# Two attention chunks ahead of the first weights, a planner that knows a shared port, and two small experts that end in one scatter

## The chip, the cores and the metric

The kernel runs on one core of a Trainium2 chip. Its engines are TensorE (PE; its weight loads are listed as PEld), VectorE (DVE), ScalarE (ACT), GpSimd (POOL) and SyncE (SP), which issues most transfers. Times are device microseconds of one execution; lower is better.

## The reference

Three stages run one after the other over 2304 rows of 512 numbers.

```python
# 1: attention with keys and values pooled by 8 (4 batches, 8 heads, 576 rows, 64 wide)
k_p = k.reshape(B, H, Sp, 8, D).mean(axis=3); v_p = v.reshape(B, H, Sp, 8, D).mean(axis=3)
attn = softmax(q @ k_p.T / 8); x = attn @ v_p           # as (2304, 512)
# 2: dense feed-forward, 512 -> 2048 -> 512
h = x @ w_in; r = np.maximum(h, 0.0); x = (r * r) @ w_out
# 3: eight experts, 512 -> 1024 -> 512; a row goes to the one with the largest logit
logits = x @ w_gate; e = argmax(logits); gate = softmax(logits)[e]
out[i] = gate[i] * (np.maximum(x[i] @ w1[e], 0.0) @ w2[e])   # first `capacity` rows of an expert; 0 for others
```

## The kernel before

**Precision.** Every large product is made from two parts of an operand, a high part rounded to the matrix format and the low rest: high by high, high by low, low by high. So each weight tile of stage 2 (32 tiles, 0 to 15 of `w_in`, 16 to 31 of `w_out`) has to be converted once, in `conv`: three steps on ACT (L265, L271, L287), three on DVE (L274 sign, L281 merge, L290 low). DVE's L290 is the last step; after it the tile can be used.

**Stages 1 and 2** work in nine chunks of 256 rows. In a chunk, attention makes scores (L412), a softmax, transposes (L499, L504) and the product with the values (L535, called av below). Stage 2 then has 16 pairs: a first-layer product `h` (L607, twelve matmuls with four `w_in` tiles), a square split into high and low (the low part on POOL, L627), and a second-layer product `y` (L640, twelve matmuls with one `w_out` tile). Chunks 0 and 1 go through stage 2 side by side, since the weights are being converted meanwhile; from chunk 2 on all weights are there.

**What sets the order.** The steps of stages 1 and 2 are not written in order. `add` records each with a priority, an engine, a cost in ns, what it reads and writes, and the buffers it takes. `Steps.run` then plays the engines through with these costs: each time it takes the step that can start earliest, the one of lowest priority number among equals, out of the first 80 of an engine's list. The order in which it took them is the order of the instructions on each engine, and each engine keeps it. A cost only decides the order; it is not a time on the chip.

**Pools at the start.** Keys are pooled on DVE (L320), laid out by ACT into `kT` (`k_place`, L363), values are pooled on DVE (L342) or, if named in `FOLD`, on POOL by three adds (L347, L348).

**The end.** After the large experts come two experts with at most 32 rows each, handled together in `twins`: `ga` makes the first layer (32 matmuls in four groups, L1446), `h_sum` turns half of it round by matmuls and relu (L1460, L1462, L1463), `gc` makes the second layer (32 matmuls, L1470), `end` scales by the gate (ACT L1481, DVE L1482) and writes the rows to their places by an indirect transfer of GpSimd, a scatter (L1485), one for each expert.

Of the kernel before, what the change touches and what calls it, by code (L numbers as in the profile page):

```python
# [58 lines left out]
COLD = 20000  # L59
FIRST = 2 * 2 * NF  # L60
PLAN_AT, W_AT, LOG7_AT = 0, 1, 6
BACK = ((3, 12, 1), (5, 12, 1))
CST2 = (6, 20)
V0_LOAD = -70
CONV_LOAD = (-30, -30, -30, -30)
# [40 lines left out]
class Step:  # L106
    def __init__(self, prio, eng, cost, fn, lat):
        self.prio, self.eng, self.cost, self.fn, self.lat = prio, eng, cost, fn, lat
        self.deps, self.bufs, self.end, self.free = set(), [], None, None


class Steps:
# [9 lines left out]
    WINDOW = 80  # L122

    def __init__(self, room, slow):
        self.room, self.slow = room, slow
        self.taken = {p: [] for p in room}
        self.steps, self.writer, self.readers = [], {}, {}

    def add(self, prio, eng, cost, fn, r=(), w=(), u=(), lat=0):
        s = Step(prio, eng, cost, fn, lat)  # L130
        for x in (*r, *w):
            if x in self.writer:
                s.deps.add(self.writer[x])
# [32 lines left out]
    def run(self):  # L166
# [6 lines left out]
        while any(todo.values()):  # L173
# [21 lines left out]
            now[e] = s.free = t + s.cost * (2 if e == "PE" and t < self.slow else 1)  # L195
# [5 lines left out]
def tile_kernel(ctx: ExitStack, tc: tile.TileContext, q, k, v, w_in, w_out, w_gate, w1, w2, cap, gate_rows, consts, out):  # L201
# [38 lines left out]
    S_ = Steps(pools, COLD)  # L240
# [8 lines left out]
    def conv(i, prio, load_prio):  # L249
# [43 lines left out]
        add(load_prio, "SP", 1320, load, w=(raw,), lat=2300)  # L293
# [5 lines left out]
        add(prio, "DVE", 605, low, r=(cv, ("W", i, 0)), w=(("W", i, 1),))  # L299
# [11 lines left out]
    def k_pool(b, x, prio, load_prio, tag=None):  # L311
# [12 lines left out]
        add(load_prio, "SP", 740, load, w=(buf,), lat=2300)  # L324
# [5 lines left out]
    def v_pool(b, i, prio, load_prio, tag=None):  # L330
# [19 lines left out]
        add(load_prio, "SP", 660 * n // P, load, w=(buf,), lat=2300)  # L350
        if ("v", b, i) in FOLD:
            add(prio, "POOL", 1600, fold, r=("ap",), w=(buf, ("v", i)))
        else:
            add(prio, "DVE", 603, pool, r=(buf, "ap"), w=(("v", i),))

    def k_place(b, prio):

        pairs = kT.rearrange("p (x a s) -> p x a s", a=2, s=SP)
        r = tuple(("kd", x) for x in range(NPAIR))

        def place(a):
            h = slice(64 * a, 64 * a + 64)
            nc.scalar.activation(out=pairs[h, :, a], in_=kd[h], func=AF.Copy, scale=1.0 / 64.0)  # L363
# [34 lines left out]
    def a_scores(c, j, prio, qprio):  # L398
# [55 lines left out]
        add(qprio, "SP", 660 * n // P, load, w=(qT,), lat=2300)  # L454
# [30 lines left out]
        if (c, j) in NORM_DVE:  # L485
            add(prio(4), "DVE", 663, lambda: norm(nc.vector), r=((mxb, 2),), w=((ex, 0), (ex, 1)), u=(mxb, ex))
        else:
            add(prio(4), "POOL", 1450 if c < 3 else 1200, lambda: norm(nc.gpsimd), r=((mxb, 2),), w=((ex, 0), (ex, 1)), u=(mxb, ex))
# [105 lines left out]
    def g1(c, ff, prio):  # L594
# [57 lines left out]
        add(prio + 1, "POOL", 1000 if c < 2 else 720, low, r=(rb, ghb), w=(glb,))  # L652
# [254 lines left out]
    def rows_of_two(cols):  # L907
# [3 lines left out]
        for e, col in enumerate(cols):  # L911
            src = idxt[0:QP, bass.ds(col, 1)]
            nc.vector.tensor_scalar_add(out=cur[0:QP, e:e + 1], in0=src, scalar1=-1.0)
            for a in range(2):
                o = slice((2 * e + a) * QP, (2 * e + a + 1) * QP)
                nc.vector.tensor_scalar(out=gix[o, 0:1], in0=src, scalar1=-1.0, scalar2=0.0, op0=ALU.add, op1=ALU.max)

# [200 lines left out]
    add(-100, "DVE", 600, start_up, w=(("kT", 0), ("kT", 1)))  # L1118
# [7 lines left out]
    for i in range(5):  # L1126
        v_pool(0, i, V0_AT, V0_LOAD, f"W{22 + i}")
# [30 lines left out]
    for c in range(NCH):  # L1158
# [34 lines left out]
        if c == NCH - 2:  # L1193
# [21 lines left out]
            add(at, "PE", 500, lambda c=c: logit_mm(c), r=(("yts", 0), ("yts", 1), "wg4"), w=(g7,), u=(yt, lgb[c]))  # L1215
# [212 lines left out]
    def twins(hooks):  # L1428
# [8 lines left out]
        sidx, gate = begin(2)  # L1437
# [3 lines left out]
        def ga(half):  # L1441
            for e in range(2):
                ps = pp.tile([P, 512], F32, tag="h", name=f"ha{half}{e}", bufs=2)
                for kk in range(KD):
                    for x in range(2):
                        nc.tensor.matmul(  # L1446
                            ps, yc[kk // 2][:, kk % 2], ws[e][2 * kk + half][:, x],
                            start=(kk == 0 and x == 0), stop=(kk == KD - 1 and x == 1),
                        )
                o = slice(HP * e, HP * e + HP)  # L1450
                if e == 0:
                    nc.scalar.copy(out=hs[half][o], in_=ps[o])
                else:
                    nc.vector.tensor_copy(out=hs[half][o], in_=ps[o])
                hook(2 * half + e)
# [11 lines left out]
        def gc(e, half):  # L1467
            for fi in range(4 * half, 4 * half + 4):
                for x in range(2):
                    nc.tensor.matmul(  # L1470
                        py[e], hx[:, fi].rearrange("p e a t -> p (e a t)"), ws[e][8 + fi][:, x],
# [3 lines left out]
        def end(e, parts):  # L1475
            hi, lo = slice(HP * e, HP * e + QP), slice(HP * e + QP, HP * e + HP)
            ot, tt = hs
            n = DM // parts
            for i in range(parts):
                c = slice(i * n, i * n + n)  # L1480
                nc.scalar.activation(out=tt[hi, c], in_=py[e][lo, c], func=AF.Copy, scale=gate[lo, 0:1])  # L1481
                nc.vector.scalar_tensor_tensor(  # L1482
                    out=ot[hi, c], in0=py[e][hi, c], scalar=gate[hi, 0:1], in1=tt[hi, c], op0=ALU.mult, op1=ALU.add
                )
            nc.gpsimd.indirect_dma_start(  # L1485
                out=out, out_offset=bass.IndirectOffsetOnAxis(ap=sidx[0:QP, e:e + 1], axis=0), in_=ot[hi], in_offset=None,
                bounds_check=NTOK - 1, oob_is_err=False,
            )
# [274 lines left out]
```

## Time and profile before

| what | us |
|---|---|
| median of 3 runs | 693.34 (692.79 to 693.70) |
| the profiled execution | 694.46 |
| its span, first to last instruction | 692.70 |
| PE busy in the span | 662.9 (96%) |
| DVE, ACT, POOL busy | 422.0, 324.9, 190.6 |

The profiled execution is 1.76 us longer than its span. PE is the engine to watch: what it does not spend on matmuls, about 30 us, lies mostly at the start and at the end. The mean shares of the others say little here, since DVE is full in one stage and half idle in the rest.

### The profile page before, as it was taken

The numbers are of one execution on the slowest core, as the hardware profiler recorded it, in microseconds if no ns is written. First come the engines' busy times: TensorE is split into PE (matmuls) and PEld (weight loads), VectorE is DVE, ScalarE is ACT, GpSimd is POOL, SyncE is SP. The second block draws the span as 40 slices with busy tenths as digits, with TensorE's granted clock in tenths as the row PEclk, the third lists the DMA queues.
The fourth block names the chain that finished last, engine by engine and source line by source line (L and its number), as shares of the span: only waits on it lengthen the run. The fifth ranks groups of instructions, "written<-read, shape, count | busy, mean of one in ns | idle before, by whom it ended". The sixth has DMA issues, their size and how long they took to land. (4 is left out here: it accounts for less than half of the span.)

```text
span 692.7 us, 11860 instructions
## 1 busy us (share of the span) xinstructions
PE 662.9 (96%) x4195; PEld 593.3 (86%) x4196; DVE 422.0 (61%) x1119; ACT 324.9 (47%) x903; POOL 190.6 (28%) x231
## 2 busy tenths in 40 slices
PE   3799999999999999999999999999999999999995
PEld 3678889999898889898898999998997979989983
DVE  5899998322279899375289647445363646464451
ACT  3897785344254243345344344243432546454351
POOL 3244433232233233234233132242202111302111
PEclk9899999999999999999999999999999999999999
DMA  9997902310122320010010000062005664553110
GB/s 311 398 400 242 312 17 68 99 63 16 61 108 64 87 77 9 1 38 19 13 48 17 2 31 1 2 226 80 1 32 185 219 222 155 190 190 130 49 58 3
DMA packets 40970, 73.46 MB, mean 106 GB/s; under 512 B 8449, under 2 KB 17921, under 8 KB 40768
## 3 DMA queue, kind: packets, MB, share of 16 engines
q1 hardware_dynamic: 38496, 64.89, 27.6%
q0 software_dynamic: 2400, 7.66, 3.4%
q8 instruction: 37, 0.61, 0.4%
q14 instruction: 37, 0.30, 0.1%
HBM read 59.63 MB, written 13.05 MB: 105 GB/s over the span
## 5 line engine op out<-in xcount | busy, mean ns | idle before, releaser
L607 PE MATMUL h<-xh,W 128*128 128x256 f32 x1152 | 213.8, 284 | 1.4 <-DVE W L290 0.8
L627 POOL TENSOR_TENSOR gl<-r,gh 128x256 fp32r<-128x256 f32 x144 | 117.2, 814 | 289.5 <-ACT gh L623 194.0
L607 PEld LDWEIGHTS h<-xh,W 128*128 128x128 f32 x1152 | 184.4, 189 | 11.7 <-DVE W L290 1.0
L640 PE MATMUL y<-W,gh 128*128 128x512 f32 x576 | 185.3, 402 | 1.3 <-DVE W L290 1.3
L607 PE MATMUL h<-xl,W 128*128 128x256 f32 x576 | 161.6, 281 | 0.2 <-DVE xl L545 0.2
L619 DVE SCALAR_TENSOR_TENSOR r<-h,r 128x256 f32<-128x256 f32 x141 | 59.1, 419 | 101.8 <-ACT r L612 101.4
L640 PE MATMUL y<-W,gl 128*128 128x512 f32 x288 | 113.8, 395 | 0.8 <-POOL gl L627 0.7
L640 PEld LDWEIGHTS y<-W,gh 128*128 128x128 f32 x576 | 99.2, 189 | 17.0 <-DVE W L290 1.9
L607 PEld LDWEIGHTS h<-xl,W 128*128 128x128 f32 x576 | 108.9, 189 | 0.4 <-DVE xl L545 0.4
L623 ACT CAST gh<-r 128x256 fp32r<-128x256 f32 x144 | 58.6, 407 | 100.1 <-DVE r L619 96.8
L612 ACT ACTIVATE r<-h 128x256 f32<-128x256 f32 x144 | 55.1, 382 | 101.2 <-PE h L607 90.0
L1334 PE MATMUL hp<-yh,W 128*128 128x256 f32 (+1 forms) x384 | 74.5, 291 | 1.1 <-issue 1.1
L697 DVE SCALAR_TENSOR_TENSOR junk<-ysb,wgb 128x512 bf16<-128x512 f32 x80 | 66.3, 829 | 1.4
L640 PEld LDWEIGHTS y<-W,gl 128*128 128x128 f32 x288 | 54.2, 188 | 14.6 <-POOL gl L627 2.0
L1334 PEld LDWEIGHTS hp<-yh,W 128*128 128x128 f32 x384 | 61.1, 188 | 1.8 <-issue 1.3
L1303 PE MATMUL po<-W,xh_e 128*128 128x512 f32 x192 | 61.4, 401 | 0.0
L1334 PE MATMUL hp<-yl,W 128*128 128x256 f32 (+1 forms) x192 | 55.7, 290 | 0.0
L233 DVE TENSOR_TENSOR W<-stg,W 128x512 fp32r<-128x512 f32 x64 | 42.3, 689 | 12.2 <-ACT W L232 11.2
L1303 PEld LDWEIGHTS po<-W,xh_e 128*128 128x128 f32 x192 | 34.7, 188 | 6.8
L1340 DVE SCALAR_TENSOR_TENSOR xl_e<-hp,xh_e 128x256 fp32r<-128x256 f32 x48 | 20.2, 422 | 31.8 <-ACT xh_e L1339 31.6
L535 PE MATMUL av<-aT,vz 128*128 128x256 f32 (+3 forms) x192 | 38.5, 352 | 0.9 <-ACT aT L509 0.9
L1292 POOL DMA_INDIRECT out_dram<-ysb,sidx x12 | 11.9, 994 | 97.5 <-ACT ysb L1281 83.1
(204 smaller groups left out, 901.4 us busy)
## 6 DMA issues: line engine op xcount, KB each, us to landing
stg<-in_moe_w_dram SPq DMA_DIRECT2D x40, 512.0 KB, 4.7
raw<-in_moe_w_in_dram SPq DMA_DIRECT2D x16, 512.0 KB, 8.3
raw<-in_moe_w_out_dram SPq DMA_DIRECT2D x16, 512.0 KB, 8.6
kraw<-in_k_dram SPq DMA_DIRECT2D x16, 288.0 KB, 3.0
out_dram<-zt SPq DMA_DIRECT2D x18, 256.0 KB, 4.6
y_dram<-ysb SPq DMA_DIRECT2D x18, 256.0 KB, 2.1
qT<-in_q_dram SPq DMA_DIRECT2D x16, 256.0 KB, 2.7
vraw<-in_v_dram SPq DMA_DIRECT2D x16, 256.0 KB, 3.9
```

The lines of the kernel that those rows point to most:

```text
L233: eng.tensor_tensor(out=lo, in0=src, in1=f(hi), op=ALU.subtract)
L535: nc.tensor.matmul(ps[:, g], vz[:, cm].rearrange("p r d -> p (r d)"), abox["aT"][:, blk, :n], start=(x == 0), stop=(x == 1),)
L607: nc.tensor.matmul(ps, wt[kk][:, l, o:o + P], r[:, kk, :], start=(n == 0), stop=(n == 3 * KD - 1))
L612: nc.scalar.activation(out=box["r"], in_=box["ps"], func=AF.Relu)
L619: nc.vector.scalar_tensor_tensor(out=r, in0=box["ps"], scalar=0.0, in1=r, op0=ALU.max, op1=ALU.mult)
L623: nc.scalar.copy(out=box["gh"], in_=box["r"])
L627: nc.gpsimd.tensor_tensor(out=box["gl"], in0=box["r"], in1=f(box["gh"]), op=ALU.subtract)
L640: nc.tensor.matmul(st["y", c][t], l[:, ts], r, start=(ff == 0 and n == 0), stop=(ff == NF - 1 and n == 2))
L697: nc.vector.scalar_tensor_tensor(out=junk, in0=st["yb", c, t] if c < 2 else st["ysb", c][t], scalar=1.0, in1=st["wgb"][:, e], op0=ALU.mult ...
L1303: nc.tensor.matmul(ps, l, r, start=(fi == 0 and x == 0), stop=(fi == 7 and x == 2))
L1334: nc.tensor.matmul(ps, ww[:, l, o], r[:, kk, 0:n2], start=(kk == 0 and x == 0), stop=(kk == KD - 1 and x == 2))
L1340: nc.vector.scalar_tensor_tensor(out=lo, in0=p_, scalar=0.0, in1=f(h), op0=ALU.max, op1=ALU.subtract)
```

## The change

The planner gets a clock for PE that falls after a pause and comes back after steady work, and lengthens a step of DVE or POOL that runs beside one of the other (for the DVE steps marked `port`). Costs are changed to suit. The attention of chunk 1 gets priorities ahead of all weights, the score products wait for their half of `kT` only, and no values are folded on POOL. `twins` puts one group of the first layer behind `h_sum(0)`, makes the second expert's result in two column halves in separate PSUM tiles, and writes both experts with one scatter over 96 partitions, of which 32 hold an index of -1 and write nothing.

```diff
-V0_LOAD = -70
-CONV_LOAD = (-30, -30, -30, -30)
+V0_LOAD = (-96,) * 5
+CONV_LOAD = (-50,) * 4
-CH1 = (0, 2, 0.5)
+CH1 = (-30, 6, 0.5)
-Q0 = {(0, 0): -98.5, (0, 1): -97, (1, 0): -50, (1, 1): -50}
-FOLD = [('v', 0, 2), ('v', 0, 3), ('v', 0, 4)]
+Q0 = {(0, 0): -98.5, (0, 1): -97, (1, 0): -95, (1, 1): -94}
+FOLD = []
...
-            now[e] = s.free = t + s.cost * (2 if e == "PE" and t < self.slow else 1)
+            cost = s.cost
+            if e == "PE":
+                if t > now[e] + self.COOL:
+                    self.warm = False
+                if t > now[e] + self.GAP:
+                    self.since = t
+                if t > self.since + self.WARM_UP:
+                    self.warm = True
+                cost *= 1 if self.warm else 2
+            if s.port:
+                o = {"DVE": "POOL", "POOL": "DVE"}[e]
+                if self.port[o] > t:
+                    cost += min(cost, self.port[o] - t) * self.SHARE[e]
+                self.port[e] = t + cost
...
-        add(prio, "DVE", 600, sign, r=(raw,), w=(cv,))
-        add(prio, "DVE", 700, merge, r=(raw,), w=(cv,))
+        add(prio, "DVE", 340, sign, r=(raw,), w=(cv,), port=True)
+        add(prio, "DVE", 605, merge, r=(raw,), w=(cv,), port=True)
...
+        parts = [slice(0, 2), slice(2, NPAIR)] if b == 0 else [slice(0, NPAIR)]
-        for a in range(2):
-            add(prio, "ACT", 450, lambda a=a: place(a), r=(*r, "ap"), w=(("kT", a), "kT in"))
+        for xs in parts:
+            cells = [g for g in range(2) if xs.start <= 2 * g < xs.stop]
+            for a in range(2):
+                w = [x for g in cells for x in (("kT", a, g), ("kT in", g))]
+                add(prio, "ACT", 450 // len(parts), lambda a=a, xs=xs: place(a, xs), r=(...), w=w)
...
-        def end(e, parts):
+        left, right = slice(0, DM // 2), slice(DM // 2, DM)
+        right_of_b = pp.tile([P, DM // 2], F32, tag="sc", name="pb", bufs=2)
+        sums = [(0, slice(0, DM), py[0]), (1, left, py[1][:, left]), (1, right, right_of_b)]
+        def end(i, tt):
...
-        ga(0)
-        ga(1)
+        ga(0, 0)
+        ga(0, 1)
+        ga(1, 0)
         h_sum(0)
+        ga(1, 1)
         gc(0, 0)
         h_sum(1)
         gc(1, 0)
+        gc(2, 0)
         gc(0, 1)
-        end(0, 1)
+        end(0, hs[1])
         gc(1, 1)
-        end(1, 2)
+        end(1, hs[1])
+        gc(2, 1)
+        end(2, yg[:, 0])
+        n = HP + QP
+        nc.gpsimd.indirect_dma_start(
+            out=out, out_offset=bass.IndirectOffsetOnAxis(ap=sidx[0:n, 0:1], axis=0), in_=hs[0][0:n], in_offset=None,
+            bounds_check=NTOK - 1, oob_is_err=False,
+        )
```

How the order of the instructions moves, at three places. On PE, from the end of chunk 1's scores to the first stage-2 product (in `ata_1_0` the first number is the chunk, the second the row tile; `h_0_0` is chunk 0, pair 0; the last number is a buffer), before:

```order
L412 MATMUL sc_1_1_0_189<-kT_86,qT_1_1_131 128x144 x2
L412 MATMUL sc_1_1_1_196<-kT_86,qT_1_1_131 128x144 x2
L499 MATMUL ata_0_0_211<-cst_60,ex_0_0_140 128x128 x4
L504 MATMUL atb_0_0_222<-cst_60,ex_0_0_140 128x128
L499 MATMUL ata_0_1_239<-cst_60,ex_0_1_161 128x128 x4
L504 MATMUL atb_0_1_249<-cst_60,ex_0_1_161 128x128
L535 MATMUL av_0_0_0_262<-aT_0_0_229,vz_89 128x256 x4
L535 MATMUL av_0_0_2_279<-aT_0_0_229,vz_89 128x256 x4
L607 MATMUL h_0_0_310<-xh_0_260,W0_220 128x256 x2
```

and after, from the transposes of chunk 0's second tile on:

```order
L520 MATMUL ata_0_1_224<-cst_60,ex_0_1_157 128x128 x4
L525 MATMUL atb_0_1_236<-cst_60,ex_0_1_157 128x128
L556 MATMUL av_0_0_0_249<-aT_0_0_206,vz_89 128x256 x4
L556 MATMUL av_0_0_2_271<-aT_0_0_206,vz_89 128x256 x4
L520 MATMUL ata_1_0_293<-cst_60,ex_1_0_210 128x128 x4
L525 MATMUL atb_1_0_306<-cst_60,ex_1_0_210 128x128
L520 MATMUL ata_1_1_311<-cst_60,ex_1_1_231 128x128 x4
L525 MATMUL atb_1_1_322<-cst_60,ex_1_1_231 128x128
L556 MATMUL av_1_0_0_332<-aT_1_0_303,vz_89 128x256 x4
L556 MATMUL av_1_0_2_350<-aT_1_0_303,vz_89 128x256 x4
L628 MATMUL h_0_0_367<-xh_0_247,W0_283 128x256 x2
```

Chunk 1's transposes and av now stand ahead of every product with weights; before they stood among chunk 0's pairs 0 to 3. On PE again, where weight tile 11 is first used (`h_0_8`; `y0_0` and `y1_0` are the two row tiles of chunk 0's second layer, here pair 7), before:

```order
L640 MATMUL y1_1_638<-W21_679,gl_1_5_921 128x512
L535 MATMUL av_2_0_0_996<-aT_2_0_941,vz_89 128x64 x8
L640 MATMUL y0_0_423<-W23_816,gh_0_7_970 128x512 x2
L640 MATMUL y0_0_423<-W23_816,gl_0_7_976 128x512
L640 MATMUL y1_0_424<-W23_816,gh_0_7_970 128x512 x2
L640 MATMUL y1_0_424<-W23_816,gl_0_7_976 128x512
L607 MATMUL h_0_8_1031<-xh_0_260,W8_860 128x256 x2
L607 MATMUL h_0_8_1031<-xl_0_261,W8_860 128x256
```

and after:

```order
L661 MATMUL y1_1_529<-W21_693,gl_1_5_915 128x512
L628 MATMUL h_0_8_991<-xh_0_247,W8_839 128x256 x2
L628 MATMUL h_0_8_991<-xl_0_248,W8_839 128x256
L628 MATMUL h_0_8_991<-xh_0_247,W9_893 128x256 x2
L628 MATMUL h_0_8_991<-xl_0_248,W9_893 128x256
L628 MATMUL h_0_8_991<-xh_0_247,W10_921 128x256 x2
L628 MATMUL h_0_8_991<-xl_0_248,W10_921 128x256
L628 MATMUL h_0_8_991<-xh_0_247,W11_968 128x256 x2
L628 MATMUL h_0_8_991<-xl_0_248,W11_968 128x256
L556 MATMUL av_2_0_0_1015<-aT_2_0_941,vz_89 128x64 x8
L661 MATMUL y0_0_465<-W23_759,gh_0_7_965 128x512 x2
L661 MATMUL y0_0_465<-W23_759,gl_0_7_970 128x512
```

The product that needs tile 11 now stands ahead of one av and one second-layer product instead of behind them. On PE in `twins` (`ha11` is the first layer's second half of expert 1, `hT0` what `h_sum(0)` makes, `po0` a result), before:

```order
L1446 MATMUL ha11_8682<-W1_258,yc0_6047 128x512 x2
L1446 MATMUL ha11_8682<-W3_294,yc0_6047 128x512 x2
L1446 MATMUL ha11_8682<-W5_530,yc1_6048 128x512 x2
L1446 MATMUL ha11_8682<-W7_617,yc1_6048 128x512 x2
L1460 MATMUL hT0_8694<-cst_60,ysb8_8_6039 128x64 x4
L1470 MATMUL po0_6049<-W24_1012,xl_e0_6053 128x512 x2
```

and after:

```order
L1481 MATMUL hT0_8680<-cst_60,ysb8_8_6035 128x64 x4
L1467 MATMUL ha11_8687<-W1_288,yc0_6043 128x512 x2
L1467 MATMUL ha11_8687<-W3_344,yc0_6043 128x512 x2
L1467 MATMUL ha11_8687<-W5_579,yc1_6044 128x512 x2
L1467 MATMUL ha11_8687<-W7_643,yc1_6044 128x512 x2
L1496 MATMUL po0_6045<-W24_973,xl_e0_6049 128x512 x2
```

One of the four groups of the first layer has moved between `hT0` and the first product that needs what comes of it.

## Rows read from the trace of the kernel before

**Rows 1.** Page: busy tenths in 40 equal slices of 17.3 us.
```profile
PE   3799999999999999999999999999999999999995
DVE  5899998322279899375289647445363646464451
```

**Rows 2.** Waits of DVE to 60 us: waited for, us in total, times, longest.
```profile
DVE kd L320 <- DMA kraw<-in_k_dram: 3.7, 3, 2.3
DVE xl L545 <- ACT xh L541: 2.3, 3, 1.3
DVE pv L342 <- DMA vraw<-in_v_dram: 1.4, 1, 1.4
DVE sm L475 <- ACT ex L439: 1.4, 1, 1.4
DVE kT L1084 <- PEq L1737: 0.9, 1, 0.9
```

**Rows 3.** Timeline of PE at the start: start, us, what, count, idle before.
```profile
9.20 6.90 PE L412 MATMUL sc<-kT,qT 128*128 128x144 f32 x32 [9.20 <-ACT kT L363]
...
22.63 6.29 PE L535 MATMUL av<-aT,vz 128*128 128x256 f32 x16 [0.90 <-ACT aT L509]
...
43.59 3.61 PE L535 MATMUL av<-aT,vz 128*128 128x256 f32 x16
```

**Rows 4.** Stretches of 2 us: length, PE busy, granted clock, DMA share, GB/s.
```profile
18.00:20.00 2.00, 0.26 (x3) 1.00 1.02 415
...
24.00:26.00 2.00, 2.00 (x6) 0.50 0.90 353
```

**Rows 5.** Timelines of POOL and DVE beside each other.
```profile
17.40 3.45 POOL L378 TENSOR_TENSOR vz<-pv,cst 128x256 f32<-128x256 f32 x4
...
19.76 0.86 DVE L274 TENSOR_SCALAR cv<-raw 128x512 uint16<-128x512 uint16 x1
...
21.92 0.45 DVE L274 TENSOR_SCALAR cv<-raw 128x512 uint16<-128x512 uint16 x1
```

**Rows 6.** Groups by line to 130 us: busy, mean ns of one.
```profile
L619 DVE SCALAR_TENSOR_TENSOR r<-h,r 128x256 f32<-128x256 f32 x27 | 11.1, 412 | 1.1 <-ACT r L612 0.8
...
L342 DVE TENSOR_REDUCE pv<-vraw 128x64 f32<-128x512 f32 x10 | 6.8, 684 | 4.8 <-DMA vraw<-in_v_dram 4.8
```

**Rows 7.** Timeline of PE around its waits of the first stage.
```profile
78.58 1.90 PE L535 MATMUL av<-aT,vz 128*128 128x64 f32 x16
...
81.77 0.40 PE L607 MATMUL h<-xh,W 128*128 128x256 f32 x2
...
83.95 0.39 PE L607 MATMUL h<-xh,W 128*128 128x256 f32 x1 [0.83 <-DVE W L290]
...
96.87 0.50 PE L640 MATMUL y<-W,gl 128*128 128x512 f32 x1 [0.71 <-POOL gl L627]
```

**Rows 8.** Timeline of all engines at the end.
```profile
676.70 2.14 PE L1470 MATMUL po<-W,xl_e 128*128 128x512 f32 x8 [1.17 <-DVE xl_e L1463]
...
679.48 5.80 PE L1470 MATMUL po<-W,xl_e 128*128 128x512 f32 x24
...
684.24 0.74 DVE L1482 SCALAR_TENSOR_TENSOR ysb<-po,gate,ysb 32x512 f32<-32x512 f32 x1 [3.68 <-ACT ysb L1481]
685.25 0.88 POOL L1485 DMA_INDIRECT out_dram<-ysb,sidx  x1 [15.97 <-DVE ysb L1482]
685.33 0.47 ACT L1481 ACTIVATE ysb<-po,gate 32x256 f32<-32x256 f32 x1 [1.12 <-PE po L1470]
...
686.84 0.48 DVE L1482 SCALAR_TENSOR_TENSOR ysb<-po,gate,ysb 32x256 f32<-32x256 f32 x1 [0.53 <-ACT ysb L1481]
688.25 0.87 POOL L1485 DMA_INDIRECT out_dram<-ysb,sidx  x1 [2.11 <-POOLq L1683]
```

**Rows 9.** Scatters by line, of 64 or 128 rows (L1292), of 32 (L1485), two answers.
```profile
L1292 POOL DMA_INDIRECT out_dram<-ysb,sidx x12: 911/1003/1021, 557.4 to 668.3; - x12
...
DMA to landing us min/median/max: 2.6/4.3/6.5
...
DMA to landing us min/median/max: 2.0/2.1/2.2
```

More of the change, by code (lines that the diff above doesn't have):

```diff
@@ L194, in run @@
                     self.taken[x.pool].append(x)
-            now[e] = s.free = t + s.cost * (2 if e == "PE" and t < self.slow else 1)
+            cost = s.cost
[12 more added lines that the diff above has]
+                self.port[e] = t + cost
+            s.at, now[e] = t, t + cost
+            s.free = now[e]
             s.end = now[e] + s.lat + self.TAIL[e]
@@ L239, in tile_kernel @@
     pools.update({f"W{i}": 1 for i in range(32)})
-    S_ = Steps(pools, COLD)
+    S_ = Steps(pools)
     add = S_.add
@@ L485, in a_scores @@
         if (c, j) in NORM_DVE:
-            add(prio(4), "DVE", 663, lambda: norm(nc.vector), r=((mxb, 2),), w=((ex, 0), (ex, 1)), u=(mxb, ex))
+            add(prio(4), "DVE", 663, lambda: norm(nc.vector), r=((mxb, 2),), w=((ex, 0), (ex, 1)), u=(mxb, ex), port=True)
         else:
-            add(prio(4), "POOL", 1450 if c < 3 else 1200, lambda: norm(nc.gpsimd), r=((mxb, 2),), w=((ex, 0), (ex, 1)), u=(mxb, ex))
+            add(prio(4), "POOL", 1110, lambda: norm(nc.gpsimd), r=((mxb, 2),), w=((ex, 0), (ex, 1)), u=(mxb, ex))
     def a_trans(c, j, aTb, abox, o, prio):
@@ L651, in g1 @@
         add(prio + 1, "ACT", 313, high, r=(rb,), w=(ghb,))
-        add(prio + 1, "POOL", 1000 if c < 2 else 720, low, r=(rb, ghb), w=(glb,))
+        add(prio + 1, "POOL", 700, low, r=(rb, ghb), w=(glb,))
         yb = ybs[c]
@@ L1116, in wgb_load @@
         st["wgb"] = wgb
-    add(-100, "DVE", 600, start_up, w=(("kT", 0), ("kT", 1)))
+    add(-100, "DVE", 600, start_up, w=[("kT", a, g) for a in range(2) for g in range(2)])
     for x in range(NPAIR):
@@ L1126, in tile_kernel @@
     for i in range(5):
[L1127 removed]
+        v_pool(0, i, V0_AT, V0_LOAD[i], f"W{22 + i}")
     for c, (at0, gap, slope) in enumerate((CH0, CH1)):
@@ L1435, in hook, with ga @@
                 fn()
-        sidx, gate = begin(2)
+        sidx, gate = begin(1)
         hs = rows_h(1)
         hx = quads(xl[0].rearrange("p (k c) -> p k c", k=8))
[L1441 to L1455, printed above, removed]
+        def ga(half, e):
+            ps = pp.tile([P, 512], F32, tag="h", name=f"ha{half}{e}", bufs=2)
+            for kk in range(KD):
+                for x in range(2):
+                    nc.tensor.matmul(
+                        ps, yc[kk // 2][:, kk % 2], ws[e][2 * kk + half][:, x],
+                        start=(kk == 0 and x == 0), stop=(kk == KD - 1 and x == 1),
+                    )
+            o = slice(HP * e, HP * e + HP)
+            if e == 0:
+                nc.scalar.copy(out=hs[half][o], in_=ps[o])
+            else:
+                nc.vector.tensor_copy(out=hs[half][o], in_=ps[o])
+            hook(2 * half + e)
         def h_sum(half):
@@ L1470, in gc @@
                     nc.tensor.matmul(
-                        py[e], hx[:, fi].rearrange("p e a t -> p (e a t)"), ws[e][8 + fi][:, x],
+                        ps, hx[:, fi].rearrange("p e a t -> p (e a t)"), ws[e][8 + fi][:, x, c],
                         start=(fi == 0 and x == 0), stop=(fi == 7 and x == 1),
                     )
-        def end(e, parts):
+        def end(i, tt):
+            e, c, ps = sums[i]
             hi, lo = slice(HP * e, HP * e + QP), slice(HP * e + QP, HP * e + HP)
[L1477 to L1487, printed above, removed]
-            )
-        ga(0)
-        ga(1)
+            nc.scalar.activation(out=tt[hi, c], in_=ps[lo], func=AF.Copy, scale=gate[lo, 0:1])
+            nc.vector.scalar_tensor_tensor(
+                out=hs[0][hi, c], in0=ps[hi], scalar=gate[hi, 0:1], in1=tt[hi, c], op0=ALU.mult, op1=ALU.add
+            )
+        ga(0, 0)
+        ga(0, 1)
+        ga(1, 0)
         h_sum(0)
+        ga(1, 1)
         gc(0, 0)
```

58 lines of the change are left out of this document (32 added, 26 removed).

## The prediction

> **What bounds the kernel now.** I read the page's 40 slices first. PE shows 9 in all slices but the first two and the last [rows 1], so the middle of the program has little for this change to win: there the products follow each other. What can move is the first stage, where weights are converted and DVE is as full as PE (8 or 9 in the slices from 17 to 121 us [rows 1]), and the last 20 us. Next I read the waits of DVE, because PE's own waits in the first stage end with DVE's work: five lines give 3.7 + 2.3 + 1.4 + 1.4 + 0.9 = 9.7 us in which DVE stood still, nearly all before 30 us [rows 2]. Then PE's timeline around its two later waits, 0.83 us for a weight tile and 0.71 us for a low part [rows 7], and last the end, instruction by instruction [rows 8].
>
> Once past its last wait of the first stage PE is full, so what it gains there reaches the end of the program undiminished. What is won behind its last product adds to that. So the sum has two parts.
>
> **The end.** Three things go.
>
> First, PE waits 1.17 us between `h_sum(0)` and `gc` [rows 8]. Now a group of the first layer stands between them. It is eight matmuls of 512 columns; `gc` takes 5.80 us for 24 such [rows 8], so eight take 1.9 us, more than the wait. The relu on ACT and DVE for which PE waited runs beside them. The wait goes: 1.17 us. For `h_sum(1)` the cover is now the first quarter of `gc`, 1.9 us too. The second expert's products become twice as many of half the width. The narrow matmuls of an av come 1.90 / 16 = 0.12 us apart [rows 7], just half of 5.80 / 24 = 0.24 [rows 8], so I take no cost; at 0.02 us each the 32 would cost 0.6, which stays in the range.
>
> Second, after the last product (679.48 + 5.80 = 685.28) ACT and DVE take turns twice, from 685.33 to 686.84 + 0.48 = 687.32, each half of the columns waiting for the one before [rows 8]. After the change the left half's turn lies beside the right half's products, and one turn is left: half of 1.99 us, 1.0 us, goes.
>
> Third, the second scatter starts at 688.25, 0.93 us after its data; the first started at 685.25, 0.27 us after DVE's 684.24 + 0.74 [rows 8]. Both write the same tensor, and the first scatter's end (685.25 + 0.88) plus a landing of 2.1 us [rows 9] is 688.2: the second waited for the first to land. With one scatter nothing is waited for: 0.66 us goes.
>
> Against that the single scatter names 96 rows instead of 32. Its issue takes between 0.87 us [rows 8] and the 1.00 us of larger ones [rows 9]; I take 0.12 more. Its landing lies between the 2.1 us of the 32-row scatters and the 4.3 us of the larger ones [rows 9]. I take 2.1, because the added entries are mostly empty or the other expert's few rows, while the larger scatters carry full rows beside other transfers; both ends stay in the range. The extra DVE instruction that writes the -1 lies under an earlier expert's products: nothing.
>
> The Trainium skill (DMA: Bandwidth & Descriptors, "Anatomy of one DMA — SWDGE (gpsimd) path") gives such a transfer about 2.0 us that do not grow with its size, so one for two is a gain at once. The 32-row scatters agree with 2.1 us, the larger ones, with 2.6 to 6.5 us, do not [rows 9]. By the page alone the landing costs nothing, as in my sum.
>
> Sum of the end: 1.17 + 1.0 + 0.66 - 0.12 = 2.7 us.
>
> **The start.** PE gets to its first weight product only when both chunks' attention is done, but the same products are then missing later, so their move alone changes nothing. What counts is when DVE has weight tiles ready. The one place where PE waited visibly for them is tile 11, until 83.95 [rows 7].
>
> DVE's waits. The waits for keys (3.7) and for the start (0.9) remain [rows 2]. Those for values and for the sums (1.4 each) and behind xl (2.3) can go, since chunk 1's softmax fills them. A new one comes: values no longer stand ahead of the first scores. The four first matmuls of the 32 that took 6.90 us last 0.9 [rows 3], and can begin about when the last key is pooled: 0.9 us. Left are 5.5 us if DVE never waits behind av, and up to 2.4 more if PE runs chunk 1's av, in which DVE's xl waits in line, at the pace of chunk 0's (6.29 us) instead of that of 43.59 (3.61) [rows 3], or a little less. I take 5.5, as the better bound is what the row of chunk 1 showed: 9.7 - 5.5 = 4.2 us saved; the other end is 1.8.
>
> DVE's work. Three pools of values come over from POOL, 3 x 0.68 = 2.05 us, and in the new order one square (0.41) more stands behind tile 11 [rows 6]: 1.64 us more. Keys and values of the second batch come ahead of tile 7, but were ahead of tile 11 before too, so they cancel here.
>
> The shared lengthening. A sign step takes 0.86 us beside POOL's vz and 0.45 alone [rows 5]. In the new order POOL's vz falls beside DVE's pools rather than its conversions: 0.41 us saved. The bounds are 0 (chunk 1's norms are on POOL beside new conversions) and 1.0 (the neighbouring steps too).
>
> So tile 11 is ready 4.2 - 1.64 + 0.41 = 2.97 us earlier, at 80.98. But PE now comes to it with one av and one y less behind it, which took from 78.58 to 81.77, 3.19 us [rows 7]. They follow it now: PE is where it was at 83.95 at 80.98 + 3.19 = 84.17, a loss of 0.2 us. If PE itself came no earlier than DVE this would all be a gain, but it does come earlier and waits. After tile 11 the counts turn (two squares, two maxima and more of the softmax then stand behind tile 27), so DVE is ahead of PE there and I let the 0.71 us for a low part [rows 7] go.
>
> Sum of the start: -0.2 + 0.7 = 0.5 us. A few steps of chunks 6 to 8 change places too; PE is full there [rows 1], and I take nothing, 0.5 us either way.
>
> **The total.** 2.7 + 0.5 = 3.2 us off. The profiled execution took 694.46 us, 692.70 in its span and 1.76 around it; it would take 691.3. The median of the runs lies 1.12 us below the profiled one, so the prediction for it is 693.34 - 3.2 = 690.1 us.
>
> **Rivals.**
>
> *DVE ahead, PE the bound (686.4).* For it: the new order puts the product with tile 11 ahead of work that was free to run, which the planner does only where it thinks the tile ready; and its step costs now come near the trace's (sign 0.45 alone). Against it: the count above. PE would then keep all that it can: chunk 0's av at the later pace, 6.29 - 3.61 = 2.7 us [rows 3], and both waits, 0.83 + 0.71 [rows 7], together 4.2; with the end 6.9 us.
>
> *Only the end (690.9 to 692.3).* DVE finds 3 us of its waits instead of 4.2, or the low part is waited for as before. The start is then -0.7 to -1.7 with or without the wait, the end 2.7: 1.0 to 2.4 us off. For it: DVE keeps its order, and both chunks' xl now stand in it ahead of conversions. Against it: by my count only chunk 1's can be late.
>
> *The scatter lands late (692.3).* At the 4.3 us of the larger scatters [rows 9] the end is worth 0.5 instead of 2.7 and the total 1.0. Against it: nothing else is in flight there.
>
> *The lower clock through both av (695.3, slower).* One mechanism: between chunk 0's av and chunk 1's, PE has only two sets of transposes to do while softmax and copies run, as it had before 20 us, when it was busy 0.26 of 2 us; after that stretch the granted clock was 0.50, the lower of the two levels, 1.2 GHz [rows 4], and the av took 6.29 us [rows 3]. If that happens ahead of chunk 1's av too, the last xl, which DVE takes in order ahead of conversions, comes 2.7 us later, and chunk 0's costs DVE a wait of 1.4 as well. DVE then saves none of its waits (9.7 - 4.6 - 0.9 - 4.1 = 0.1), tile 11 comes at 83.95 + 1.64 - 0.1 = 85.5 and PE loses 85.5 + 3.19 - 83.95 = 4.7 us against the 2.7 at the end: 2.0 us slower. It decides the sign once tile 11 is later than 83.5. Against it: the two av now stand closer together, and the first scores ran at the upper level from PE's first work on.
>
> The Trainium skill (TensorE: Matmul & The Clock Gate, "Part 1: The HAM clock gate (the "warmup" mystery)") has the lower level as the state without activity, lifted by steady work: by that rule, each pause added ahead of the first long run speaks for this rival. The stretch from 24 us agrees (0.50 [rows 4]); that the clock stood at 1.00 before, while PE was nearly idle, does not.
>
> **How the numbers follow.** Chances: the forecast 0.42, PE the bound 0.25, only the end 0.20, late landing 0.08, the lower clock 0.05. Less than 0.2% (1.4 us, from 691.95 to 694.73) cannot be told from no change here. Faster is all of the first two, most of the third and some of the fourth: 0.84; the same 0.12; slower 0.04. The likeliest case by itself spans 688.8 to 691.2 (contention 0 to 1.0, the low part's wait, 0.5 in the middle, part of DVE's waits). The range for 8 in 10 goes on to the bound of PE below and to the late landing above: 686.0 to 692.2.
>
> **What would show it.** At the end: one scatter that starts about 1.3 us after PE's last product instead of 3.0, and no wait of PE after `h_sum(0)`. At the start: DVE's waits to 60 us at 5.5 to 6.5 us; a wait of PE for a weight tile at the eighth pair that is longer than 0.83 us and ends near 81; the 0.71 us gone. I am wrong if PE shows no wait for weights there (then the first rival), if chunk 1's av runs at the lower clock, or if the span ends more than 5 us after the scatter starts (it was 4.45).

## The result and the profile after

| | before | after |
|---|---|---|
| median of runs, us | 693.34 (690.94 to 694.24) | 686.72 (686.09 to 687.05) |
| ratio, 95% interval | | 0.9905 (0.9891 to 0.9919) |
| span of the profiled execution, us | 692.70 | 684.80 |
| start of the first product with weights, of `twins`, end of PE | 28.58, 667.09, 685.28 | 34.94, 662.02, 678.94 |

The change took 6.6 us off, where 3.2 were forecast. The spans differ by 7.9 us: 2.8 lie behind the start of `twins` (25.61 us to the end before, 22.78 after), as forecast (2.7); 5.07 lie ahead of it, where 0.5 was forecast. The total is that of the rival "DVE ahead, PE the bound" (686.4).

**Where the 5.07 us were.** The busy time of the engines by stretch, of the kernel before. The columns: length, then PE, PE's weight loads, DVE, ACT and POOL busy (instructions), granted clock, DMA share, GB/s. The length minus the first busy time is what PE stood still.

```profile
0.00:28.00 28.00, 13.96 (x55) 11.74 (x57) 19.00 (x36) 14.86 (x31) 9.66 (x22) 0.88 0.95 341
28.00:36.00 8.00, 7.23 (x52) 6.34 (x51) 7.24 (x15) 7.12 (x19) 2.40 (x3) 1.00 1.04 411
36.00:60.00 24.00, 22.69 (x136) 19.35 (x135) 22.88 (x46) 22.54 (x50) 9.45 (x8) 1.00 0.83 323
60.00:86.00 26.00, 25.17 (x166) 22.56 (x166) 25.26 (x42) 19.01 (x43) 11.17 (x13) 1.00 0.99 311
86.00:130.00 44.00, 43.28 (x279) 38.87 (x279) 37.19 (x68) 28.74 (x68) 16.56 (x19) 1.00 0.25 66
130.00:400.00 270.00, 268.75 (x1765) 242.76 (x1764) 164.10 (x489) 109.76 (x399) 81.07 (x103) 1.00 0.13 41
```

The same stretches after:

```profile
0.00:28.00 28.00, 15.10 (x68) 12.68 (x69) 21.84 (x47) 16.25 (x38) 7.74 (x15) 1.00 0.96 338
28.00:36.00 8.00, 7.36 (x24) 6.11 (x25) 6.28 (x17) 5.86 (x13) 0.00 (x0) 0.59 1.04 407
36.00:60.00 24.00, 24.00 (x163) 21.76 (x163) 23.29 (x43) 23.61 (x53) 9.34 (x9) 1.00 0.80 289
60.00:86.00 26.00, 25.68 (x165) 22.40 (x163) 24.64 (x44) 22.20 (x50) 11.06 (x12) 1.00 1.05 339
86.00:130.00 44.00, 44.00 (x287) 39.85 (x286) 33.53 (x62) 24.53 (x60) 15.42 (x18) 1.00 0.26 74
130.00:400.00 270.00, 270.00 (x1779) 244.82 (x1778) 165.22 (x490) 112.61 (x401) 84.81 (x104) 1.00 0.13 41
```

PE's idle time fell by 1.14, 0.13, 1.31, 0.51, 0.72 and 1.25 us: 5.06 in all, as much as the difference at the start of `twins` (from 400 us to there it is 2.35 before and 2.57 after). It lay in six stretches with a little in each. The slices of [rows 1] show a 9 throughout the last four of them, since a 9 is 90% or more.

PE's waits before, from its first weight product (28.58) to 400 us (waited for, us, times, longest):

```profile
PE y L640 <- DVE W L290: 1.3, 2, 1.1
PE h L607 <- DVE W L290: 0.8, 1, 0.8
PE y L640 <- POOL gl L627: 0.7, 1, 0.7
PE ata L499 <- POOL ex L451: 0.7, 1, 0.7
PE h L607 <- ACT r L612: 0.5, 1, 0.5
PE pi L840 <- DVE s_ic L803: 0.5, 1, 0.5
PE h L607 <- DVE xl L545: 0.2, 1, 0.2
```

They are 4.7 us. After, from 34.94 to 400 us, there is one wait, the 0.20 us at tile 11 below.

**The places of [rows 2 to 4].** DVE's waits to 60 us after; the five largest lines give 8.3 us against 9.7, and these three are among them:

```profile
DVE kd L337 <- DMA kraw<-in_k_dram: 3.8, 3, 2.1
DVE xl L566 <- ACT xh L562: 1.7, 2, 1.1
DVE mx L442 <- PE sc L432: 1.3, 1, 1.3
```

PE's timeline at the start (start, us, what, count, idle before) and the stretch that answers to the second of [rows 4]:

```profile
20.56 3.72 PE L556 MATMUL av<-aT,vz 128*128 128x256 f32 x16 [1.56 <-ACT aT L530]
...
28.64 6.64 PE L556 MATMUL av<-aT,vz 128*128 128x256 f32 x16 [0.69 <-ACT aT L530]
```

```profile
28.00:30.00 2.00, 1.35 (x3) 1.17 (x4) 1.99 (x6) 2.00 (x6) 0.00 (x0) 0.50 1.06 401
```

Chunk 0's av now runs at the upper clock (3.72 instead of 6.29 us) and chunk 1's at the lower (6.64 instead of 3.61): 2.57 us gained and 3.03 lost, so the clock gave nothing between the two in this execution.

**Tile 11 [rows 7].** PE's timeline after:

```profile
78.14 0.38 PE L628 MATMUL h<-xh,W 128*128 128x256 f32 x1 [0.20 <-DVE W L307]
...
78.48 1.89 PE L556 MATMUL av<-aT,vz 128*128 128x64 f32 x16
```

The wait is 0.20 us and ends at 78.1, where a longer one ending near 81 was forecast; the wait for a low part is gone.

**The end [rows 8, 9].** All engines after, then the new scatter's landing:

```profile
667.61 1.00 PE L1481 MATMUL hT<-cst,ysb 128*128 128x64 f32 x8
668.42 2.09 PE L1467 MATMUL ha<-W,yc 128*128 128x512 f32 x8
...
670.35 2.04 PE L1496 MATMUL po<-W,xl_e 128*128 128x512 f32 x8
...
677.84 1.10 PE L1496 MATMUL pb<-W,xl_e 128*128 128x256 f32 x8
...
679.48 0.48 DVE L1505 SCALAR_TENSOR_TENSOR ysb<-pb,gate,yg 32x256 f32<-32x256 f32 x1 [0.37 <-ACT yg L1504]
680.24 0.93 POOL L1525 DMA_INDIRECT out_dram<-ysb,sidx  x1 [16.01 <-POOLq L1712]
```

```profile
DMA to landing us min/median/max: 2.4/2.4/2.4
```

No wait stands behind `hT`, and the scatter starts 0.28 us after its data (679.48 + 0.48) and 1.30 us after PE's last product (677.84 + 1.10 = 678.94).

### The profile page after: what moved, and what is told of

Its sections match the earlier page's. It is cut to its first block, busy times and chain, and to the rows that moved or that the text cites. A ratio compares the mean times of both kernels' runs of the same rounds, so it can differ in the third digit from the quotient of the medians.

```text
span 684.8 us, 11897 instructions
## 1 busy us (share of the span) xinstructions
PE 662.5 (97%) x4211; PEld 595.3 (87%) x4212; DVE 419.8 (61%) x1123; ACT 326.6 (48%) x905; POOL 186.7 (27%) x221
## 5 line engine op out<-in xcount | busy, mean ns | idle before, releaser
L718 DVE SCALAR_TENSOR_TENSOR junk<-ysb,wgb 128x512 bf16<-128x512 f32 x80 | 68.5, 856 | 1.4
```

Of the source, the lines that this page charges most:

```text
L718: nc.vector.scalar_tensor_tensor(out=junk, in0=st["yb", c, t] if c < 2 else st["ysb", c][t], scalar=1.0, in1=st["wgb"][:, e], op0=ALU.mult ...
```

## The experiments

Each ran in five rounds against the kernel before (medians 693.3 to 693.7). Ratios have their 95% interval behind them. They ran in batches on four chips (e1 to e4, e5 to e8, e9 to e11, e12); between batches the ratios say more than the medians.

### End and start apart

**e1**, only the end: the kernel before with the new `twins`.

```diff
-        ga(0)
-        ga(1)
+        ga(0, 0)
+        ga(0, 1)
+        ga(1, 0)
         h_sum(0)
+        ga(1, 1)
...
-        end(1, 2)
+        end(1, hs[1])
+        gc(2, 1)
+        end(2, yg[:, 0])
```

> The kernel before with the new `twins` alone (and its index rows): order and costs of stages 1 and 2 stay. The step 'the end' of the prediction asks for 2.7 us off, 690.6; its rival 'the scatter lands late' for 0.5 off, 692.8. If the whole gain of 6.6 us sat in the end (theory 'end'), it would be 686.7.

691.14 us, 0.9962 (0.9950 to 0.9975): 2.6 us off. The trace has again 22.78 us from the start of `twins` (665.62) to the end of the span (688.4). The step "the end" holds.

**e2**, only the start: the kernel after with the old `twins`, so e1's diff the other way round.

> The kernel after with the old `twins`: planner, costs, priorities and folds are new, the end is old. The prediction's step 'the start' (what counts is when tile 11 is ready) asks for 0.5 us off, 692.8. Theory 'waits' (every wait of PE after its first weight product goes, 4.7 us in the trace of before against 0.2 in the trace after) asks for 4.0 to 4.7 off, 688.6 to 689.3, and PE waits from the first weight product to 300 us of under 0.5 us.

688.43 us, 0.9924 (0.9912 to 0.9936): 5.3 us off. From the first weight product (33.28) to 300 us PE has no wait at all. The theory "waits" holds, and the forecast of 0.5 for the start is off by its size. (2.6 + 5.3 is 1.3 more than both together gave; the three intervals together allow that, and it stays open.)

### The place of the attention or the planner's costs

**e3**, the attention at its old place under the new planner:

```diff
-CH1 = (-30, 6, 0.5)
+CH1 = (0, 2, 0.5)
...
-FOLD = []
+FOLD = [('v', 0, 2), ('v', 0, 3), ('v', 0, 4)]
```

(Q0, V0_LOAD and CONV_LOAD as before, too.)

> The kernel after with the old priorities (CH1, Q0, V0_LOAD, CONV_LOAD) and the old FOLD: planner, costs and `twins` are the new ones, chunk 1's attention stands among chunk 0's pairs again. Theory 'place' (the attention ahead of the weights is what takes PE's waits away) asks for the start's 4 us back, 690 to 691. Theory 'costs' (the planner's new step costs and its rule for the shared port order DVE's work better, wherever the attention stands) asks for 686.7 to 688, with under 1 us of PE waits for W, gl, r and xl after the first weight product.

**e4**, the opposite: new priorities and no folds in the kernel before.

```diff
-V0_LOAD = -70
-CONV_LOAD = (-30, -30, -30, -30)
+V0_LOAD = -96
+CONV_LOAD = (-50, -50, -50, -50)
...
-CH1 = (0, 2, 0.5)
+CH1 = (-30, 6, 0.5)
```

(Q0 and FOLD as after, too.)

> The kernel before with the new priorities and no folds: old planner, old costs, old `twins`. Theory 'place' asks for 4 us off, 689.3. Theory 'costs' asks for 692 to 695, with PE waiting for W as before or longer (the old planner takes a sign step for 0.60 us and a merge for 0.70, and lets DVE run beside POOL without a price).

e3: 690.70 us, 0.9955 (0.9941 to 0.9969), which beside e1 leaves 0.5 us for the new planner alone. e4: 692.06 us, 0.9985 (0.9973 to 0.9998), 1.0 us for the place alone. Neither theory holds: together they are worth 5.3. In e3 PE reaches its first weight product at 23.96, eleven us earlier than after, and soon waits for what the other engines have not finished. PE's waits in e3 from there to 400 us (waited for, us, times, longest):

```profile
PE ata L520 <- ACT aT L530: 1.9, 1, 1.9
PE h L628 <- DVE W L307: 1.3, 2, 1.0
PE y L661 <- POOL gl L648: 1.1, 1, 1.1
PE h L628 <- DVE xl L566: 0.7, 1, 0.7
PE h L628 <- ACT W L304: 0.6, 1, 0.6
```

Behind the pauses for xl and W, which end at 25 to 29 us, the granted clock was 0.50 from 28 to 34 us. In e4 the 2.8 us of waits for W, r and xl behind the first weight product (35.11) are gone as after, but the old order of POOL and DVE keeps 0.8 us of waits for a low part, 0.7 for POOL's softmax and 0.3 for an index there, 1.8 against 1.9 before. So in these traces the place takes one part of the waits away and the planner the other. That does not explain how little e4 gave: its profiled execution (690.97) lies 1.1 us below its median, and what the slower ones waited for is not shown.

**e6**, the new costs without the rule for the shared port:

```diff
-    SHARE = {"DVE": 0.7, "POOL": 0.5}
+    SHARE = {"DVE": 0.0, "POOL": 0.0}
```

> The kernel after with SHARE at 0 for both engines: the planner keeps the new priorities, costs and PE clock, but not the rule that lengthens DVE and POOL beside each other. If that rule is what gives DVE its lead over PE, PE waits for W, gl or xl again and 2 us or more come back (688.7 or more). If the new costs (sign 0.34, merge 0.605 us) and the place of the attention are enough, it is 686.4 to 687.4 with under 0.5 us of such waits.

695.09 us, 1.0026 (1.0013 to 1.0038): with the new end in it, the start has lost all its gain and 4 us more. Four stretches of e6:

```profile
36.00:60.00 24.00, 24.00 (x158) 21.48 (x157) 23.65 (x44) 22.84 (x52) 10.51 (x9) 1.00 0.80 270
60.00:86.00 26.00, 25.04 (x159) 21.22 (x158) 24.15 (x46) 23.34 (x51) 11.43 (x13) 1.00 1.00 320
86.00:130.00 44.00, 42.36 (x272) 37.81 (x272) 28.91 (x56) 23.32 (x57) 15.61 (x18) 1.00 0.32 92
130.00:400.00 270.00, 265.83 (x1746) 239.77 (x1745) 164.28 (x487) 109.30 (x396) 80.70 (x101) 1.00 0.13 41
```

PE is full to 60 us, so tile 11 is not the matter; 4.17 us are lost from 130 to 400, for instance 1.42 us at 225 and 1.40 at 321 in which PE waits for POOL's softmax. The old planner carried the lengthening in its fixed costs (0.60 for a sign, 1.2 to 1.45 for POOL's softmax step); the new one has the bare costs and needs the rule to know it.

### Does POOL lengthen DVE?

In the trace of before a sign step begins beside POOL's softmax step and ends 0.33 us behind its end (33.40 + 1.49 = 34.89; 33.80 + 1.42 = 35.22), just the 0.34 us that a sign step alone keeps the next one waiting (21.92 to 22.26 in the same trace):

```profile
33.40 1.49 POOL L451 TENSOR_TENSOR ex<-ex,sm 128x576 f32<-128x576 f32 x1 [12.55 <-issue]
```

```profile
33.80 1.42 DVE L274 TENSOR_SCALAR cv<-raw 128x512 uint16<-128x512 uint16 x1
```

So it did nothing until POOL was done. (The next long sign agrees: it ends at 37.58 + 1.34 = 38.92, 0.32 us behind a softmax step of POOL that ends at 37.00 + 1.60.) The Trainium skill (SBUF — State Buffer, "SBUF: two separate sides") calls the port pair that the two share an exclusive lock, in which the later of the two fully blocks; these rows agree.

DVE's groups up to tile 11's low step, before (to 83.89 us): busy, mean ns of one, idle before.

```profile
L290 DVE TENSOR_TENSOR W<-cv,W 128x512 fp32r<-128x512 f32 x20 | 15.4, 776 | 0.3 <-ACT W L287 0.2
L274 DVE TENSOR_SCALAR cv<-raw 128x512 uint16<-128x512 uint16 x22 | 14.1, 660 | 0.0
...
L342 DVE TENSOR_REDUCE pv<-vraw 128x64 f32<-128x512 f32 (+1 forms) x7 | 4.8, 682 | 2.0 <-DMA vraw<-in_v_dram 1.9
```

And after (to 78.09 us):

```profile
L307 DVE TENSOR_TENSOR W<-cv,W 128x512 fp32r<-128x512 f32 x20 | 13.6, 696 | 0.6 <-ACT W L304 0.6
L291 DVE TENSOR_SCALAR cv<-raw 128x512 uint16<-128x512 uint16 x22 | 11.0, 527 | 0.0
L359 DVE TENSOR_REDUCE pv<-vraw 128x64 f32<-128x512 f32 (+1 forms) x10 | 6.7, 670 | 1.2 <-DMA vraw<-in_v_dram 1.2
```

The same 22 signs and 20 lows took 3.1 and 1.8 us less; the 21 merges took as long as before (16.2 and 16.3 us). **e9** puts the lengthening back: one more POOL step on a scratch tile behind each low part.

```diff
             nc.gpsimd.tensor_tensor(out=box["gl"], in0=box["r"], in1=f(box["gh"]), op=ALU.subtract)
+            if c < 2 and ff < 8:
...
+                nc.gpsimd.tensor_tensor(out=st["junk"], in0=st["junk"], in1=st["junk"], op=ALU.subtract)
```

> The kernel after with one more GpSimd step (128x240, on a scratch tile that nothing else uses, about 0.7 us) behind each low part of chunks 0 and 1, pairs 0 to 7: 16 steps, some 11 us of GpSimd, with nothing new for VectorE and the same order there. Theory 'lengthening' (in the trace before, DVE's sign and low steps up to tile 11 cost 0.58 and 0.71 us a step against 0.44 and 0.62 after, which with the smaller terms is 4.4 us of the 5.8 us by which tile 11 is earlier; the cause is GpSimd beside them): DVE's sum of work to tile 11 grows from 68.4 us by 3 to 6 us, PE waits at tile 11 for most of it, 689 to 692. If the lengthening has another cause (DVE's own order or the transfers), DVE's sum stays within 0.5 us and the total within 1 us of 687.4, but for a low part that comes late (a PE wait for gl in the trace would show it).

687.73 us, 0.9923 (0.9904 to 0.9942). DVE's groups up to tile 11 (77.73 us) in e9:

```profile
L307 DVE TENSOR_TENSOR W<-cv,W 128x512 fp32r<-128x512 f32 x20 | 15.8, 804 | 0.0
L291 DVE TENSOR_SCALAR cv<-raw 128x512 uint16<-128x512 uint16 x22 | 12.7, 604 | 0.0
```

They took 2.2 and 1.7 us more than after, by POOL steps alone: the lengthening is real, and it is POOL's. The total moved by only 1.0 us from e5's (below) by the ratios, though, which their intervals do not tell from nothing. DVE's later waits (3.5 us behind 20 us in the trace after) vanished, so tile 11 was ready at 77.73. The longer steps filled the 1.2 us for values; the 1.7 us behind xl may have another cause, since chunk 1's av ran at the upper clock here (3.72 us) and there is no such wait in e8, which has that too. PE waited 1.20 us at tile 11, 0.21 at another tile and 0.54 for a low part. The first half of the theory is shown; the price in the end is smaller than expected.

### Who is ahead at tile 11

**e5** is the kernel after, unchanged.

> The kernel after, unchanged, as the base for e6 to e8 on the same chip: 686.7 by its earlier runs. In its first trace chunk 0's av ran at the upper clock (3.72 us) and chunk 1's at the lower (6.64); in e2, whose stages 1 and 2 are the same program, 4.09 and 5.25, the first weight product came at 33.28 instead of 34.94 us, and `twins` began 2.1 us earlier. If PE bounds the stages (theory 'waits'), the start of `twins` minus the start of the first weight product is again 626.6 to 627.1 us, whatever the two av took.

687.44 us, 0.9908 (0.9889 to 0.9927). First weight product 33.23, `twins` 660.80: 627.6 us between, against 626.6 to 627.1 expected, and PE waited 0.75 us at tile 11. So an earlier PE meets DVE there: of the 1.7 us by which it came earlier than in the trace after, 1.2 reached `twins`.

**e7** puts 2.4 us more on DVE just ahead of tile 11; **e8** keeps PE busy between the two av.

```diff
-            nc.vector.tensor_tensor(out=W[i][:, 1], in0=f(box["a"]), in1=f(W[i][:, 0]), op=ALU.subtract)
+            for _ in range(3 if i in (9, 10) else 1):
+                nc.vector.tensor_tensor(out=W[i][:, 1], in0=f(box["a"]), in1=f(W[i][:, 0]), op=ALU.subtract)
```

```diff
+                if c == 1 and i == 0:
+                    for _ in range(8 if j == 0 else 2):
+                        nc.tensor.transpose(a[:, 0, :n], ident[:n, :n], ident[:n, :n])
                 nc.tensor.transpose(a[:, i, :n], e[:n, i * P:(i + 1) * P], ident[:n, :n])
...
+            if c == 1:
+                for _ in range(4):
+                    nc.tensor.transpose(a[:, 3, :n], e[:n, 3 * P:4 * P], ident[:n, :n])
...
-            nc.tensor.transpose(box["tb"][:, :n], e[:n, NROW - P:NROW], ident[:n, :n])
+            for _ in range(5 if c == 1 else 1):
+                nc.tensor.transpose(box["tb"][:, :n], e[:n, NROW - P:NROW], ident[:n, :n])
```

> The kernel after with the low step of weight tiles 9 and 10 done three times on DVE instead of once: four more steps of 0.60 us, 2.4 us of DVE just ahead of tile 11, with the same order. The prediction's account (tile 11's readiness on DVE sets PE) asks for +2.2 to 2.4 us, 689, as a wait of PE at tile 11. Theory 'waits' in its strong form (DVE has a lead of some us) asks for 0 to 0.5. The wait of 0.20 at tile 11 in the first trace speaks for the former; that DVE's tile 11 came 1.7 us earlier in e2, where PE was earlier too, says that DVE itself follows PE there, and may speak for the latter.

> The kernel after with PE kept busy between the two av: ten more transposes ahead of chunk 1's, and each last transpose repeated four times behind it, which write what they wrote before. They lie in PE's waits of 1.04, 0.60 and 0.69 us there, and change no result. If chunk 1's av then runs at the upper clock (3.7 us instead of 6.6), PE reaches the first weight product 2.5 to 3 us earlier. Theory 'waits' (PE the bound): the total falls by as much, 683.7 to 684.5. The prediction's account (DVE sets tile 11): PE waits there as much longer, 686.5 to 687. If the clock falls all the same, 686.7 to 687.5.

e8: 686.61 us, 0.9897 (0.9877 to 0.9916), no difference from e5 that can be told. Chunk 1's av ran in 3.72 us, but the added transposes took up most of that: the first weight product came at 33.11, 1.83 us earlier than in the trace after and only 0.12 earlier than in e5's. PE waited 1.05 us at tile 11, so nothing of it shows in the total; as a test of who leads, the run is weak. e7: 691.61 us, 0.9970 (0.9954 to 0.9987), 4.2 more than e5 for a dose meant as 2.4 us of DVE. PE's timeline in e7, and a stretch:

```profile
75.63 0.51 PE L629 MATMUL h<-xh,W 128*128 128x256 f32 x2 [1.65 <-DVE r L641]
...
78.30 0.58 PE L629 MATMUL h<-xh,W 128*128 128x256 f32 x1 [1.04 <-DVE W L308]
...
78.90 3.51 PE L557 MATMUL av<-aT,vz 128*128 128x64 f32 x16
```

```profile
80.00:82.00 2.00, 2.00 (x12) 2.00 (x11) 2.00 (x3) 1.28 (x3) 1.68 (x3) 0.50 1.15 347
```

On DVE the dose was nearer 3 us: from the start of the last pooled part to that of tile 11's low step it took 9.48 us (68.10 to 77.58) against 6.53 in e5 (69.78 to 76.31). PE stood still for 2.7 us, and behind that the clock fell: the av took 3.51 instead of 1.89 us and what followed ran at 0.50 too. The product with tile 11 came 1.26 us later than in e5 (78.30, 77.04) and `twins` 4.2 us later (665.00, 660.80), so 2.9 of the 4.2 us were lost behind tile 11. DVE thus had no lead in the kernel after that would have hidden the dose. PE waited at tile 11 for 0.20 (after), 0.75 (e5), 1.05 (e8), 1.20 (e9) and no time (e2): the two meet there within about a us, and both accounts, "DVE sets it" and "PE is the bound", were half right.

**e10** gives DVE a lead: the last part of the second batch's values, for whose transfer DVE waited 1.1 to 2.5 us at 70 us, is pooled behind tile 11. **e11** adds e8's edit, **e12** e7's.

```diff
-at + step * x, at + step * (x - 3))
+at + step * (x + (8 if (b, x) == (1, 9) else 0)), at + step * (x - 3))
```

> The kernel after with the last part of the second batch's values pooled behind tile 11's low step on DVE instead of ahead of tile 9: DVE waited there 1.1 to 2.5 us for that transfer (69 to 71 us) in e2, e5, e8 and the kernel after. PE's order is the same. If DVE sets tile 11 whenever PE comes early (e5 and e8 waited 0.75 and 1.05 us there), tile 11 comes 1 to 2 us earlier and these waits go: 0.3 to 0.8 off 687.4. If PE is the bound in most executions: no change.

> e10 together with e8: PE reaches the first weight product some 2 us earlier on the mean, since chunk 1's av always runs at the upper clock, and DVE has tile 11 ready 1 to 2 us earlier. Theory 'PE and DVE meet at tile 11, so each alone brings nothing and both together do': 1 to 2 us off, 685.5 to 686.5. If another wait stands right behind (the next tiles, chunk 2's av), 686.6 as e8.

> e10 with the dose of e7 (the low step of tiles 9 and 10 three times, 2.4 us of DVE ahead of tile 11). In e10's trace tile 11's low part is there some 1.6 us before PE asks for it (75.72). If this lead is real, most of the dose disappears in it: PE waits 0.8 us at tile 11 or for the square behind the dose, the clock stays up, 685.5 to 686.5. If DVE has no lead in e10 either (its gain came from elsewhere), the dose costs what it cost in e7, 4 us: 689.

e10: 685.01 us, 0.9879 (0.9859 to 0.9899), some 2 us below the kernel after. Its interval just overlaps those of the kernel after (0.9891 to 0.9919, and e5's 0.9889 to 0.9927); e11's below does not. In its trace PE has no idle time from 28 to 400 us, for instance:

```profile
60.00:86.00 26.00, 26.00 (x173) 23.41 (x172) 25.71 (x48) 23.90 (x54) 12.09 (x13) 1.00 1.05 343
```

A trace of e2, whose stages 1 and 2 are those of the kernel after, was as good (no wait, `twins` at 659.91 against 660.31 in e10), so e10's gain shows in the medians and not in the best execution. e11: 684.76 us, 0.9869 (0.9850 to 0.9887), the same as e10; the two are the fastest versions. e12: 687.11 us, 0.9901 (0.9885 to 0.9918): the dose that cost 4.2 us in e7 cost 1.5 here by the ratios (2.1 by the medians; the intervals overlap a little), with 0.93 us of waiting at tile 11 and the clock at 1.00 behind it. That is between the two expectations: the lead is there, and smaller than the dose.

## Why the prediction was right in direction and wrong in size

**The end** was right term by term: 1.27 us less on PE (1.17 forecast), 1.02 less from the last product to the data (1.0), 0.65 from the waiting scatter (0.66), 0.06 more for the issue (0.12). The landing took 2.4 instead of 2.1 us, of which the span shows 0.05 (3.58 us behind the issue before, 3.63 after). Together that is 2.83 us.

**The start** failed, at the sentence "The one place where PE waited visibly for them is tile 11" and at the sum that hung on it, -0.2 for tile 11 and 0.7 for the low part. In that sum tile 11 gave 83.95 - (78.14 + 3.19) = 2.6 us, the low part its 0.7, and the waits behind chunk 2, taken as nothing, 1.2: 4.5 of the 5.07. The other half us is not traced to one place. Three parts of the sum were wrong:

- *Places left out.* The sum took two waits of PE [rows 7]. From its first weight product to 400 us PE waited 4.7 us before and 0.2 after: beside those two also 1.3 for W (until 39.87 and 42.32 us), 0.7 for r and xl, and 1.2 at chunks later than 2, which the prediction set to nothing because the slices [rows 1] show a 9. All of them went.
- *The shared lengthening.* Taken as 0.41 us, with 1.0 as its bound, from one sign step [rows 5]. Signs and lows alone gave 4.9 us, and e9 puts 3.9 of it back with POOL steps alone. It is the term of DVE's sum that was mis-sized by most: seven rows of signs up to tile 11 are longer than alone in the trace of before, not one. What it was worth in time is less: e9 lost 1.0 us by it, and that is not clear of the noise.
- *DVE's waits.* 4.2 us were to go; 1.4 went (9.7 to 8.3 us to 60 us). Chunk 1's av did run at the lower clock, so xl kept 1.7 of its 2.3 us, and the scores' 1.3 us (0.9 forecast) took the place of the values' 1.4.

Tile 11 was thus ready at 78.1 instead of the 80.98 forecast, though DVE's added pools were sized well (1.9 more against 2.05). PE's two steps behind it, 3.19 us, were right too.

**The rivals.** "DVE ahead, PE the bound" has the right total (686.4), with 0.20 us left of its two waits, but not by its clock term of 2.7 us, and DVE was not ahead (e5, e7); that its total fits is luck. The measured time lies in the range only because the lower end was set for this rival. "The lower clock through both av" came half true (chunk 1's), one of the signs that the prediction named against itself, without the loss that the rival forecast. What it cost is open: in e5 and e2 that av was 1.4 us shorter and `twins` began 1.2 and 2.1 us earlier, while e8, with the av at the upper clock, gained nothing. The ground against this rival, that the first scores ran at the upper level, is not borne out: the clock is printed as 1.00 there, but PE did six scores a us from 10 to 13 us and nine from 14 to 16. "The scatter lands late" did not come: 0.3 of 2.2 us.

What stays open: why place and costs, worth 1.0 and 0.5 us alone, are worth 5.3 together is shown by their traces only as far as the waits go. e6 shows that the port rule is needed with the new costs, but no run takes it away in the first stage alone, where the forecast failed; in e6 most of the loss lies behind 130 us.

## What to carry to other kernels

Before a stage is called full, sum what its engine does not do (length minus busy, stretch by stretch): some 1 us of idle time in each of several stretches hides under a row of nines. Where two engines lengthen each other, count how many steps stand in the other's shadow instead of pricing one, and put the lengthening into the plan once, as a rule or as a cost (e6 has neither and is slower than before). A lead of one engine over another is measured by a dose: what a known delay costs tells how much of it was covered. How long the delay really was has to be read from the trace (e7: about 3 us, not 2.4).

## What the runs showed that was not expected

- Waits of 1.65 and 1.04 us, 2.7 us apart, dropped PE's granted clock to 0.50 (e7); a single wait of 0.93 (e12) or 1.20 (e9) did not. That is why a dose of some 3 us of DVE cost 4.2.
- The same work up to chunk 1's av gives that av 6.64, 5.27 or 3.72 us (the kernel after, e5, e7): the clock of this stretch differs from execution to execution. With PE kept busy between the two av it took 3.72 both times (e8, e11), but so it did in e7 and e9 without that, so it is not shown that the added transposes did it.
- A profiled execution can stand 1 us beside the median: the first weight product of the kernel before came at 28.58 in one and at 27.43 in e1, whose first two stages are the same program.
